# Attention, soft mixture and gated layer on one core: logit sums, combine products and batch-end steps on other engines and in other places

## The chip, the cores and the metric

One core of one Trainium2 chip runs the whole program in one launch. The metric is the device time of one execution in microseconds (us). The engines are named as the profile names them: PE is TensorE, which multiplies matrices (PEld is its weight load), DVE is VectorE, ACT is ScalarE, POOL is GpSimd, and SP is SyncE, whose queue issues the DMAs.

## What is computed

Three layers follow each other, all in float32. The input is q, k, v of 4 batches, 8 heads, 1152 positions, 64 wide; neighbouring pairs of queries are averaged first, so that 576 queries are left for each head.

```
q_pool = q.reshape(B, H, S // 2, 2, D).mean(axis=3)
attn = softmax(q_pool @ k.T / sqrt(D)); x = (attn @ v), heads side by side: 2304 x 512
logits = x @ phi                                  # phi: 512 x 32 slots
d = softmax over tokens of logits;  slot_input = d.T @ x
slot_out[e] = relu(slot_input[e] @ w1[e]) @ w2[e]  # 8 experts, 4 slots each
c = softmax over slots of logits (1e-9 added to the sum);  x = c @ slot_out
out = (silu(xn @ w_gate) * (xn @ w_val)) @ w_out   # xn: x over its rms, times rms_g
```

The part that the change touches is the softmax of the logits: `d` runs over all tokens and is made batch by batch with a running maximum, `c` runs over the 32 slots of one token.

## The kernel before, in words

The attention runs over 16 head pairs, p = 0 to 15, four to a batch; a stage is the work of one pair. Its loop has nine visits, kt = 0 to 8, one for each block of 128 keys. In a visit `qk` (L412) makes the scores of both halves (h = 0, 1) of the 288 + 288 queries on TensorE in four products, the last of which subtracts each query's maximum, and ScalarE makes the exponentials (L423). `add_e` (L428) adds the exponentials up on GpSimd in two accumulators a half (kt = 0 to 4 and 5 to 8), and `av` (L440) makes the output's products, three blocks of keys in every third visit. In p = 0 and 15 (`HALVED`) VectorE makes part of the sums, and the two halves follow each other. The maxima of later pairs are made in the same loop: `wide_item` (L354) makes scores on TensorE in a two-bank tile, VectorE reduces them.

All score-like results share one PSUM tag, `u`, of three two-bank tiles, which `two_banks` (L241) gives out; `bank` (L244) takes one of these for any smaller result too. A new tile takes the place of the one that was released longest ago in the order of the program, and waits until its last reader is done.

The order on each engine is written out by hand. `STEP` and `STEP_V` (L31, L32) list the steps of a visit (every third one is a `STEP_V`, of ten steps: scores q0 and q1, a maximum m, sums e0 and e1, the output's products a, b, c, with two more maxima between a and b). `side(p)` (L765) collects the steps at the side of a stage, each with a due time from `AT` (or `AT_0`, `AT_15` and `AT_01`, which replace some of its times in certain stages): a time of 5.46 means that the step's instructions are issued ahead of the first step of the visit kt = 5 that begins at 0.46 of it or later. So a due time sets the place of an instruction in the queue of its engine, and an engine takes its queue in order.

The steps at the side that matter here, for the pair l = p - 1 that has just been finished:

- `sum_up` (L456, due 0.1 and 0.11) adds the two accumulators of each half on VectorE. `turn_64` (L759, due 0.9, 5.76, 5.77) turns a 512-wide block of 64-bit weights into float32 on VectorE (L756). `sums` (L460, 2.75) adds over the keys on TensorE and ScalarE adds 1e-9; `recips` (L474) turns and inverts.
- `x_turn_all` (L499, 8.75) turns the outputs on TensorE; `x_divide` (L507, 8.76 and 8.77) divides them on VectorE. With `AT_01`, in stages with p > 1 and p % 4 < 2, these are due at 8.85 to 8.87.
- `x_logits` (L517, 5.45) makes the pair's share of the logits on TensorE in a `u` tile; `logit_mul` (L525, 5.46) divides it on VectorE; `logit_add` (L531, 6.3) adds it to the batch's logits on VectorE. It does so for the second to fourth pair of a batch: eleven times in the loop.
- `max_red` and `max_row` (L382, L385, 5.75 and 5.95) finish the maxima of the next pair and turn them to a row; `send_row` (L392, 6.0) sends it by DMA. `low_k` (L325, 6.1 and 6.2) makes the low part of the next keys on VectorE.
- At the end of a batch (p = 4, 8, 12) `d_turn` (L551) and `d_exp` (L578) make the exponentials over the tokens; for two halves VectorE then adds the two sums (L585). A stage later (p = 5, 9, 13) `d_back`, `d_copy`, `slot_part`, `slot_copy` and `slot_turn` (L587 to L633) follow. In p = 6, 10, 14 `c_turn` (L644) starts the combine's softmax of the batch, in p = 7, 11, 15 `c_exp` and `c_soft2` (L657, L660) end it: exponential on ScalarE; sum, addition of 1e-9 from the tile `eps`, inverse and product on VectorE. For the last batch these run ahead of the experts (L1130 to L1132).
- `pair_up` (L637, in p = 2) fills two constant tiles on VectorE.

After the loop come the last logits, the experts (L1014 on) and the gated layer (L1176 on), which TensorE fills almost alone.

Of the kernel before, what the change touches and what calls it, by code (L numbers as in the profile page):

```python
# [7 lines left out]
F32 = mybir.dt.float32  # L8
# [5 lines left out]
AF = mybir.ActivationFunctionType  # L14
ALU = mybir.AluOpType
# [3 lines left out]
NP = 16  # L19
# [31 lines left out]
    d_back=2.76,  # L51
    d_copy=2.77,
# [4 lines left out]
    c_soft=6.5,  # L57
# [9 lines left out]
    x_logits=5.45,  # L67
    logit_mul=5.46,
# [39 lines left out]
    take_x=0.24,  # L108
    sum_up=[0.25, 0.26],
# [52 lines left out]
def attention_softmoe_gated_kernel(ctx: ExitStack, tc: tile.TileContext, kT, qT, vv, ip, cst, w1, w2, wg, wv, wo, rg, out):  # L162
# [105 lines left out]
    eps = one.tile([TB, NBK], F32, name="eps")  # L268
# [262 lines left out]
    def logit_add(p):  # L531
        b, hp = divmod(p, 4)
        if hp:
            dv.tensor_tensor(out=lg[b], in0=lg[b], in1=srow[p], op=ALU.add)
        rel("B")
# [42 lines left out]
    def d_exp(g, o, nm):  # L578
        n = len(o)
        dtx[g] = B([32, 576], F32, "dtx")  # L580
        sm = S([32, 2], "sm")
        for h in range(n):
            ac.activation(dtx[g][:, HQ * h:HQ * h + HQ], o[h], AF.Exp, bias=nm, accum_out=sm[:, h:h + 1] if n > 1 else sall[:, g:g + 1])
        if n > 1:
            dv.tensor_tensor(out=sall[:, g:g + 1], in0=sm[:, 0:1], in1=sm[:, 1:2], op=ALU.add)  # L585
# [51 lines left out]
    def pair_up():  # L637
        dv.memset(pair, 0.0)
        dv.memset(eps, 1e-9)
        for h in range(2):  # L640
            r = slice(64 * h, 64 * h + 64)
            dv.tensor_copy(pair[r, h], stack[r, 0:32])
# [17 lines left out]
    def c_soft2(b):  # L660
        t = ct[b]
        sm = S([TB, NBK], "csm")
        dv.reduce_sum(out=sm, in_=t, axis=AX.X)
        dv.tensor_tensor(out=sm, in0=sm, in1=eps, op=ALU.add)
        dv.reciprocal(sm, sm)
        dv.tensor_tensor(out=cn[:, NBK * b:NBK * b + NBK, :], in0=t, in1=sm[:, :, None].to_broadcast([TB, NBK, 32]), op=ALU.mult)
# [98 lines left out]
    def side(p):  # L765
# [3 lines left out]
        def at(name, g):  # L769
            ts = (AT_0 if p == 0 else AT_15 if p == NP - 1 else AT_01 if p > 1 and p % 4 < 2 else AT).get(name, AT.get(name))  # L770
            for i, t in enumerate(ts if isinstance(ts, list) else [ts]):
                todo.append((t, len(todo), (lambda i=i: g(i))))
# [20 lines left out]
        if l >= 0:  # L793
# [14 lines left out]
            if p % 4 == 1 and p > 1:  # L808
                b = p // 4 - 1
                at("d_back", lambda i: d_back(b))  # L810
# [7 lines left out]
            if p % 4 == 3 and p > 3:  # L818
                b = p // 4 - 1
                at("c_exp", lambda i: c_exp(b))  # L820
                at("c_soft", lambda i: c_soft2(b))
# [27 lines left out]
    with tc.manual_schedule():  # L849
# [282 lines left out]
        c_soft2(3)  # L1132
# [216 lines left out]
```

## Time and profile before

| | us |
|---|---|
| median of 3 runs | 748.03 (747.66 to 750.51) |
| profiled execution | 744.76 |
| its span, first to last instruction | 742.9 |
| PE busy | 699.8 (94%) |
| DVE busy | 478.8 (64%) |
| POOL busy | 422.5 (57%) |
| ACT busy | 391.3 (53%) |

The span is read from the trace of the profiled execution; all times of single instructions are from it, in us from its first instruction. "Busy" counts the time in which an engine works on instructions; an instruction that has been started and is held up by another engine's access to the memory counts as busy, and so shows as a long instruction. The granted TensorE clock was 0.993 of the full one.

### The profile page before, as it was taken

What the parts mean: (1) busy time and instruction counts of PE and PEld (TensorE: products, weight loads), DVE (VectorE), ACT (ScalarE), POOL (GpSimd) and SP (SyncE); (2) the same over time, 40 slices, a digit from 0 to 9 for tenths busy, and PEclk for the clock granted to TensorE, in tenths of its full rate; (3) what the DMA queues carried; (4) which work ended last, traced back from release to release, by engine and by line L of the source; (5) the groups of instructions that cost most, each with busy time, mean ns of one, the idle gap of its engine ahead of it and who ended that gap; (6) DMA issues with size and microseconds to landing.
All of it is one profiled execution on the core that took longest, in us unless ns stands there. A gap on an engine that the chain in (4) does not pass through costs nothing.

```text
span 742.9 us, 15218 instructions
## 1 busy us (share of the span) xinstructions
PE 699.8 (94%) x5967; PEld 487.7 (66%) x5967; DVE 478.8 (64%) x691; ACT 391.3 (53%) x809; POOL 422.5 (57%) x340
## 2 busy tenths in 40 slices
PE   4999989899999899999999998989999999999998
PEld 2666656566666566666665665544357888888887
DVE  5968898887787887687897674432053755544420
ACT  2455656566656556565665543432155856554320
POOL 5336877876777677678777665221016854535330
PEclk9999999999999999999999999989999999999999
DMA  5221642844636617427416306079990010000001
GB/s 173 96 88 64 210 153 73 265 134 163 231 123 209 223 59 252 177 67 276 153 44 225 137 11 230 29 258 363 398 401 26 15 44 29 28 30 15 28 29 43
DMA packets 52855, 103.56 MB, mean 139 GB/s; under 512 B 5816, under 2 KB 19632, under 8 KB 52784
## 3 DMA queue, kind: packets, MB, share of 16 engines
q1 hardware_dynamic: 52784, 102.59, 39.6%
q8 instruction: 47, 0.77, 0.4%
q14 instruction: 24, 0.20, 0.1%
HBM read 89.39 MB, written 13.11 MB: 138 GB/s over the span
## 4 chain that ended last, share of the span: by engine, by line
PE 73%; DVE 13%; issue 5%; DMA 4%; ACT 3%; POOL 2%; SPq 0%; ACTq 0%; DVEq 0%; POOLq 0%
PE yo L1252 20%; PE sc L421 16%; PE av L444 15%; DVE mx L365 4%; PE mxp L364 4%; PE gv L1204 3%; DMA w<-away 2%; POOL acc L438 2%; DVE mx L371 2%; ACT e L423 2%; PE sums L469 1%; PE mxp L374 1%; PE hin L1021 1%; PE xl L521 1%; PE xo L504 1%
## 5 line engine op out<-in xcount | busy, mean ns | idle before, releaser
L438 POOL TENSOR_TENSOR acc<-acc,e 128x576 f32<-128x576 f32 x148 | 205.6, 1415 | 59.3 <-ACT e L423 49.9
L423 ACT ACTIVATE e<-sc 128x576 f32<-128x576 f32 x288 | 166.4, 657 | 93.2 <-PE sc L421 90.9
L365 DVE TENSOR_REDUCE mx<-mxp 128x2 f32<-128x1024 f32 x120 | 143.7, 1222 | 55.5 <-PE mxp L364 55.4
L444 PE MATMUL av<-e,vt 128*64 128x288 f32 x1152 | 165.2, 415 | 0.0
L438 POOL TENSOR_TENSOR acc<-e 128x576 f32<-128x576 f32 x60 | 91.9, 1549 | 95.3 <-ACT e L423 88.4
L444 PEld LDWEIGHTS av<-e,vt 128*64 128x64 f32 x1152 | 73.4, 136 | 60.5 <-issue 22.8
L421 PE MATMUL sc<-qh,kh 64*128 64x288 f32 x576 | 97.9, 329 | 3.6 <-DVE xt L513 2.8
L1252 PE MATMUL yo<-woh,hA 128*128 128x512 f32 (+1 forms) x312 | 98.9, 384 | 0.0
L421 PE MATMUL sc<-mr,pick 64*128 64x288 f32 x576 | 88.3, 294 | 1.5 <-DMA mr<-mrow 1.5
L421 PE MATMUL sc<-ql,kh 64*128 64x288 f32 x576 | 87.8, 294 | 0.0
L421 PE MATMUL sc<-qh,kl 64*128 64x288 f32 x576 | 87.7, 294 | 0.0
L1209 DVE SCALAR_TENSOR_TENSOR th<-th,gv 128x384 f32<-128x384 f32 x72 | 39.9, 554 | 62.5 <-ACT th L1206 61.9
L421 PEld LDWEIGHTS sc<-qh,kh 64*128 64x128 f32 x576 | 55.8, 185 | 28.9 <-issue 9.4
L1235 POOL TENSOR_TENSOR hA<-hu,hA 128x384 fp32r<-128x384 f32 x48 | 48.7, 1016 | 43.0 <-ACT hA L1234 39.3
L1252 PEld LDWEIGHTS yo<-woh,hA 128*128 128x128 f32 x312 | 57.6, 188 | 10.2 <-issue 0.7
L421 PEld LDWEIGHTS sc<-mr,pick 64*128 64x128 f32 x576 | 57.2, 187 | 1.9 <-DMA mr<-mrow 1.9
L1252 PE MATMUL yo<-wol,hA 128*128 128x512 f32 (+1 forms) x151 | 57.9, 383 | 0.0
L1206 ACT ACTIVATE th<-gv 128x384 f32<-128x384 f32 x72 | 35.2, 488 | 42.4 <-PE gv L1204 39.1
L421 PEld LDWEIGHTS sc<-qh,kl 64*128 64x128 f32 x576 | 57.1, 189 | 0.2
L421 PEld LDWEIGHTS sc<-ql,kh 64*128 64x128 f32 x576 | 56.9, 187 | 0.0
L364 PE MATMUL mxp<-kh,qh 64*128 64x512 f32 x240 | 49.1, 437 | 0.0
L1211 DVE SCALAR_TENSOR_TENSOR hu<-th,gv 128x384 f32<-128x384 f32 x72 | 39.9, 555 | 8.4 <-DVE th L1209 0.4
(201 smaller groups left out, 1070.9 us busy)
## 6 DMA issues: line engine op xcount, KB each, us to landing
w<-in_w_dram SPq DMA_DIRECT2D x86, 256.0 KB
w<-in_w_dram SPq DMA_DIRECT2D x21, 512.0 KB
vt<-in_vv_dram SPq DMA_DIRECT2D x16, 576.0 KB
qraw<-in_qT_dram SPq DMA_DIRECT2D x15, 576.0 KB
kraw<-in_kT_dram SPq DMA_DIRECT2D x15, 576.0 KB
away<-w SPq DMA_DIRECT2D x32, 256.0 KB
w<-away SPq DMA_DIRECT2D x32, 256.0 KB
raw<-in_wg_dram SPq DMA_DIRECT2D x12, 512.0 KB
```

What stands on the lines that cost most here:

```text
L364: pe.matmul(o[:, s, :], lhsT=q[r, 128 * t:128 * t + 128], rhs=k[r, 512 * c:512 * c + 512], start=True, stop=True)
L365: dv.reduce_max(out=heads[:, :, t, c], in_=o, axis=AX.X)
L421: pe.matmul(o[:, s, 0:HQ], lhsT=w[r, wk], rhs=q[r, c], start=(i == 0), stop=(i == 3))
L423: ac.activation(ets[p, kt, h], o[:, :, 0:HQ], AF.Exp, scale=0.0625)
L438: eng.tensor_tensor(out=acc[p, h, j], in0=first[p, h, j] if n == 1 else acc[p, h, j], in1=e, op=ALU.add)
L444: pe.matmul(avt[p, h][64 * s:64 * s + 64, 0:HQ], lhsT=vt[p][:, kt, 64 * s:64 * s + 64], rhs=ets[p, kt, h][:, s], start=(kt == 0), stop=(kt ...
L1204: pe.matmul(o[i], lhsT=sg[n][:, 256 * i + 128 * c:256 * i + 128 * c + 128], rhs=cT[g], start=True, stop=True)
L1206: ac.activation(t, o[0], AF.Tanh, scale=0.5)
L1209: dv.scalar_tensor_tensor(out=t, in0=t, scalar=1.0, in1=o[0], op0=ALU.add, op1=ALU.mult)
L1211: dv.scalar_tensor_tensor(out=u, in0=t, scalar=0.5, in1=o[1], op0=ALU.mult, op1=ALU.mult)
L1235: gp.tensor_tensor(out=b, in0=u, in1=f(a), op=ALU.subtract)
L1252: pe.matmul(o, lhsT=x, rhs=w[:, c], start=(ft == 0 and i == 0), stop=(ft == NF - 1 and i == 2))
```

## The change

The due times of eight steps change, `logit_add` and `pair_up` go from VectorE to GpSimd, the sum behind `d_exp` becomes a step `d_sum` of its own, and `c_soft2` becomes two steps: `c_sum`, in which ScalarE adds the 1e-9 between two instructions of VectorE, and `c_out`, the product, on GpSimd in the loop and on VectorE for the last batch. `AT_01` now holds in stages with p % 4 = 2 too.

```
 AT:     d_back 2.76 -> 2.81, d_copy 2.77 -> 2.82, new d_sum=2.8
         c_soft 6.5 -> [6.5, 8.9]
         x_logits 5.45 -> 5.78, logit_mul 5.46 -> 5.785
 AT_15:  new c_soft=[3.9, 4.6]
@@ logit_add
-            dv.tensor_tensor(out=lg[b], in0=lg[b], in1=srow[p], op=ALU.add)
+            gp.tensor_tensor(out=lg[b], in0=lg[b], in1=srow[p], op=ALU.add)
@@ d_exp
-        if n > 1:
-            dv.tensor_tensor(out=sall[:, g:g + 1], in0=sm[:, 0:1], in1=sm[:, 1:2], op=ALU.add)
+        dpart["s", g] = sm
+
+    def d_sum(g):
+        sm = dpart.pop(("s", g))
+        dv.tensor_tensor(out=sall[:, g:g + 1], in0=sm[:, 0:1], in1=sm[:, 1:2], op=ALU.add)
@@ pair_up
-        dv.memset(pair, 0.0)
-        dv.memset(eps, 1e-9)
+        gp.memset(pair, 0.0)
         for h in range(2):
             r = slice(64 * h, 64 * h + 64)
-            dv.tensor_copy(pair[r, h], stack[r, 0:32])
+            gp.tensor_copy(pair[r, h], stack[r, 0:32])
@@ c_soft2
-    def c_soft2(b):
-        t = ct[b]
-        sm = S([TB, NBK], "csm")
-        dv.reduce_sum(out=sm, in_=t, axis=AX.X)
-        dv.tensor_tensor(out=sm, in0=sm, in1=eps, op=ALU.add)
+    def c_sum(b):
+        sm = csum[b] = S([TB, NBK], "csm")
+        dv.reduce_sum(out=sm, in_=ct[b], axis=AX.X)
+        ac.activation(sm, sm, AF.Copy, bias=1e-9)
         dv.reciprocal(sm, sm)
-        dv.tensor_tensor(out=cn[:, NBK * b:NBK * b + NBK, :], in0=t, in1=sm[:, :, None].to_broadcast([TB, NBK, 32]), op=ALU.mult)
+
+    csum = {}
+
+    def c_out(b, eng=gp):
+        eng.tensor_tensor(out=cn[:, NBK * b:NBK * b + NBK, :], in0=ct[b], in1=csum[b][:, :, None].to_broadcast([TB, NBK, 32]), op=ALU.mult)
@@ side
-            ts = (... AT_01 if p > 1 and p % 4 < 2 else AT)...
+            ts = (... AT_01 if p > 1 and p % 4 < 3 else AT)...
             if p % 4 == 1 and p > 1:
+                at("d_sum", lambda i: d_sum(b))
             if p % 4 == 3 and p > 3:
-                at("c_soft", lambda i: c_soft2(b))
+                at("c_soft", lambda i: (c_sum, c_out)[i](b))
@@ ahead of the experts
-        c_soft2(3)
+        c_sum(3)
+        c_out(3, dv)
```

## Rows read from the trace of the kernel before

**Rows 1.** The page, part 1: busy us (share of the span) and instructions of each engine.

```profile
PE 699.8 (94%) x5967; PEld 487.7 (66%) x5967; DVE 478.8 (64%) x691; ACT 391.3 (53%) x809; POOL 422.5 (57%) x340
```

**Rows 2.** Waits of PE: who waited for whom: us in total, times, longest us.

```profile
PE xo L504 <- DVE mx L365: 5.9, 5, 2.3
...
PE mxt L388 <- DVE mxw L383: 4.1, 13, 1.0
PE sums L469 <- DVE acc L457: 2.9, 2, 1.7
PE sums L469 <- DVE mx L365: 2.9, 2, 2.4
PE sc L421 <- DVE xt L513: 2.8, 3, 0.9
...
PE dn L591 <- DVE mx L365: 1.4, 3, 0.5
```

**Rows 3.** Groups of instructions on DVE, shapes apart: count | busy us, mean ns | idle before.

```profile
L534 DVE TENSOR_TENSOR lg<-lg,srow 128x288 f32<-128x288 f32 x11 | 14.9, 1355 | 0.0
...
L529 DVE TENSOR_TENSOR srow<-xl,srow 128x288 f32<-128x288 f32 x11 | 4.9, 448 | 0.0
...
L666 DVE TENSOR_TENSOR cn<-ct,csm 96x192 f32<-96x192 f32 x4 | 4.2, 1050 | 0.1
...
L642 DVE COPY pair<-cs 64x32 f32<-64x32 f32 x2 | 2.6, 1278 | 0.0
```

**Rows 4.** Timeline of DVE, p = 6, kt = 5 and 6: start us, us, instruction [idle before].

```profile
211.73 1.23 DVE L365 TENSOR_REDUCE mx<-mxp 128x2 f32<-128x1024 f32 x1 [0.57 <-PE mxp L364]
...
214.12 0.18 DVE L383 TENSOR_REDUCE mxw<-mx 128x9 f32<-128x27 f32 x1
214.22 1.28 DVE L756 SCALAR_TENSOR_TENSOR w<-w,raw 128x512 uint32<-128x512 uint32 x2
215.42 1.42 DVE L328 TENSOR_TENSOR kl<-kraw,kh 128x576 fp32r<-128x576 f32 x2
216.76 1.69 DVE L534 TENSOR_TENSOR lg<-lg,srow 128x288 f32<-128x288 f32 x1
```

**Rows 5.** Timeline of POOL, p = 6: the two accumulations of kt = 6.

```profile
216.25 3.46 POOL L438 TENSOR_TENSOR acc<-e 128x576 f32<-128x576 f32 x2 [3.21 <-ACT e L423]
```

**Rows 6.** Timeline of POOL, first accumulations of p = 2, 3, 4, 5, 7, 8, 12.

```profile
82.56 3.39 POOL L438 TENSOR_TENSOR acc<-e 128x576 f32<-128x576 f32 x2 [1.19 <-ACT e L423]
...
112.00 2.80 POOL L438 TENSOR_TENSOR acc<-e 128x576 f32<-128x576 f32 x2 [2.90 <-ACT e L423]
...
138.59 3.47 POOL L438 TENSOR_TENSOR acc<-e 128x576 f32<-128x576 f32 x2 [0.51 <-ACT e L423]
...
169.75 2.90 POOL L438 TENSOR_TENSOR acc<-e 128x576 f32<-128x576 f32 x2 [2.65 <-ACT e L423]
...
227.14 2.80 POOL L438 TENSOR_TENSOR acc<-e 128x576 f32<-128x576 f32 x2 [1.96 <-ACT e L423]
...
256.10 2.80 POOL L438 TENSOR_TENSOR acc<-e 128x576 f32<-128x576 f32 x2 [2.84 <-ACT e L423]
...
369.35 3.29 POOL L438 TENSOR_TENSOR acc<-e 128x576 f32<-128x576 f32 x2 [1.44 <-ACT e L423]
```

**Rows 7.** Timeline of PE, p = 6: output products a, the turned maxima, scores of kt = 6.

```profile
210.11 1.14 PE L444 MATMUL av<-e,vt 128*64 128x288 f32 x8
...
214.45 0.30 PE L388 MATMUL mxt<-cs,mxw 128*128 128x128 f32 x1 [0.27 <-DVE mxw L383]
...
215.32 0.29 PE L421 MATMUL sc<-qh,kh 64*128 64x288 f32 x2
```

**Rows 8.** Timeline of DVE, end of p = 4.

```profile
166.44 0.66 DVE L585 TENSOR_TENSOR sall<-sm 32x1 f32<-32x1 f32 x1 [1.19 <-ACT dtx L583]
```

**Rows 9.** Groups on POOL, shapes apart: the sum of 192 columns.

```profile
L877 POOL TENSOR_TENSOR qs<-qraw 128x192 f32<-128x192 f32 x1 | 0.6, 589 | 1.1 <-DMA qraw<-in_qT_dram 1.1
```

**Rows 10.** Timeline of ACT, p = 7, kt = 6 to 8: the exponentials.

```profile
243.50 3.41 ACT L423 ACTIVATE e<-sc 128x576 f32<-128x576 f32 x6 [0.47 <-PE sc L421]
```

More of the change, by code (lines that the diff above doesn't have):

```diff
@@ L50 @@
     sums=2.75,
-    d_back=2.76,
-    d_copy=2.77,
+    d_sum=2.8,
+    d_back=2.81,
+    d_copy=2.82,
     max_tail=[2.85, 2.86],
@@ L56 @@
     c_exp=0.9,
-    c_soft=6.5,
+    c_soft=[6.5, 8.9],
     pair_up=6.6,
@@ L66 @@
     slot_copy=5.77,
-    x_logits=5.45,
-    logit_mul=5.46,
+    x_logits=5.78,
+    logit_mul=5.785,
     logit_add=6.3,
@@ L108 @@
     take_x=0.24,
+    c_soft=[3.9, 4.6],
     sum_up=[0.25, 0.26],
@@ L267, in attention_softmoe_gated_kernel @@
     pair = one.tile([128, 2, 32], F32, name="pair")
-    eps = one.tile([TB, NBK], F32, name="eps")
     rgt = one.tile([128, 4], F32, name="rgt")
@@ L769, in at @@
         def at(name, g):
-            ts = (AT_0 if p == 0 else AT_15 if p == NP - 1 else AT_01 if p > 1 and p % 4 < 2 else AT).get(name, AT.get(name))
+            ts = (AT_0 if p == 0 else AT_15 if p == NP - 1 else AT_01 if p > 1 and p % 4 < 3 else AT).get(name, AT.get(name))
             for i, t in enumerate(ts if isinstance(ts, list) else [ts]):
```

## The prediction

> **What bounds the kernel now.** I read the page first: TensorE is busy for 94% of the span, VectorE and GpSimd for 64% and 57% [rows 1]. So the time is TensorE's own work plus the gaps in it, and a change that touches only the other engines can win no more than the gaps. I then read who makes TensorE wait [rows 2]. In the sixteen stages of the attention (one a head pair, p = 0 to 15) the gaps made by VectorE are: the turned outputs, 5.9 in five gaps (2.2 in p = 2, 2.3 in p = 7, 0.44, 0.44 and 0.49 in p = 6, 10, 11); the turned maxima, 4.1 in thirteen; the sums, 2.9 behind a maximum (2.4 in p = 4, 0.5 in p = 2) and 2.9 behind the accumulators' sum in p = 15; the scores behind x_divide, 2.8 in three (p = 5, 9, 13); d_back, 1.4 in the same three.
>
> Next I asked why VectorE is late. Eight of the eleven logit sums take 1.69 and three 0.45, the two copies of pair_up 1.28 each, the combine's product 1.05 on average [rows 3]. In p = 6, GpSimd's accumulation starts 0.5 us ahead of the slow sum, and the sum ends 0.3 after it [rows 4, 5]; that accumulation and the next one last 3.46 together, where two alone take 2.80 (p = 3) [rows 5, 6]. So the engines hold each other up a whole instruction at a time, and the one that waits goes next. VectorE's time is lost to GpSimd's sums, and the change trades this one way for the other.
>
> The last view is the start of each stage. VectorE adds the accumulators as soon as GpSimd has made its last one, then turns a weight (0.64, as in [rows 4]), and only then makes the maxima that TensorE's sums wait for. GpSimd starts on the new stage when the second exponentials are there; the idle time before that is the room VectorE has [rows 6]. The accumulators' sum is two instructions of 0.7. A room of 1.4 holds both, and the weight gets in ahead of GpSimd: in p = 12 the room is 1.44 and TensorE waits for nothing. In p = 2 it is 1.19, the weight comes behind one of GpSimd's sums, and TensorE waits 0.5. In p = 4 it is 0.51, the second instruction comes behind GpSimd too, and TensorE waits 2.4. So the limits are about 1.4 and 0.7.
>
> **The change, part by part** (us; plus is longer).
>
> Gaps that go. The 2.2 in p = 2 goes: the sum (1.69) and pair_up (its copies 2.6, and the memsets) leave VectorE. The 2.3 and 0.49 in p = 7 and 11 go: VectorE is rid of the sum, the addition of 1e-9 and the product. The two 0.44 in p = 6 and 10 go, as x_turn stands eight matmul instructions of the output products, or 1.1, later [rows 7]. Sum -5.9. In p = 5, 9, 13 VectorE no longer waits 1.19 for the exponentials and 0.66 in the tiny d_sum [rows 8], 1.85 against gaps of 0.93: -2.8. There d_back too stands behind 1.1 more of products, against gaps of 0.47: -1.4. The moved d_sum (0.66) is covered by the time in which TensorE makes d_back and then the products of VectorE's next maximum; uncovered it would cost its 0.66 three times. No DMA is moved: send_row, load_v and SP's queue keep their places, and the row leaves 0.3 earlier.
>
> Logits behind the maxima. TensorE no longer makes xl ahead of the last maxima, so VectorE's idle 0.57 goes and the maxima end 0.57 earlier. The gap of 0.27 ahead of the turned maxima goes in eleven stages: -2.9. But xl takes one of three score buffers, and the second pair of scores of kt = 6 now needs it back, behind the product, which stands behind max_red and two weights. In p = 6: the product starts at 215.42 - 0.57 = 214.85, ends 0.45 later at 215.30 [rows 3, 4], and with 0.14 to signal (as from mxw to mxt) the scores start at 215.44. TensorE would be there 0.27 ahead of the 215.32 of before [rows 7], so it waits 0.39. Eight stages turn two weights there: +3.1. With one weight (p = 1, 11, 14) the product is 0.6 earlier: nothing. In p = 5, 9, 13 slot_part's sixteen matmul instructions stand ahead of xl and give VectorE time: nothing there (at most the 0.39).
>
> Logits' sum on GpSimd. The trace has no such sum; GpSimd's sums take 0.59 at 192 columns and 1.40 at 576 [rows 6, 9]; in proportion between them 288 columns take 0.79. These are the bounds, and I take 0.79. It waits behind the product, and the accumulation of kt = 6 waits behind it. It becomes ready during the first low_k (0.71 each), so it goes between the two: the second low_k and that accumulation come 0.79 - 0.12 = 0.67 later. GpSimd no longer waits 0.3 for VectorE's sum, so its last accumulation ends 0.35 to 0.45 later, TensorE's scores 0.12 later: the room of the next stage shrinks by 0.3.
>
> By the Trainium skill, GPSIMD Engine Reference, section 4.1 (Engine selection), an elementwise sum belongs on VectorE, GpSimd being about twice as slow with two inputs. By that the sum would take 0.90 and the room would shrink by a further 0.1, worth some 0.2 in the total.
>
> Combine. In p = 7 and 11 VectorE makes the sum, ScalarE adds 1e-9, VectorE inverts. ScalarE would come to its copy after two of the six exponentials that now run back to back [rows 10], at 244.65; VectorE ends its sum behind both low_k, in p = 7 at 243.28 (product) + 0.71 + 0.79 + 0.71 + 0.34, or 245.8. So the exponentials behind the copy are held 1.3, three score buffers run full, and TensorE stands for it (VectorE's inverse waits too, but only the maxima of kt = 8 queue behind it, whose products come later): +1.3 in p = 7, +1.1 in p = 11, where one weight is turned. If low_k were not split it would be 0.45 each. In p = 15, where both have idle time, nothing (at most the 1.3). The product itself (0.59 by the 192-column sum, up to 1.0) goes to GpSimd behind its last accumulation, and the accumulators' sum waits for it: 0.6 less room in p = 8 and 12. In the experts' phase the same hop stands against an addition and a product that held VectorE up: nothing, within 0.3 either way.
>
> What is late next: the rooms. GpSimd's work behind kt = 6 is one unbroken row of accumulations, so whatever TensorE stops waiting there comes off the next room:
> - p = 3: 2.90 - 0.3 - 2.2 - 0.7 for pair_up on GpSimd (three small instructions without a row, between nothing and three times 0.59; I take 0.7, nearer the low end as they are 32 and 64 columns wide) is below zero. GpSimd goes straight on, and a third instruction of VectorE's comes behind one of its sums, 1.4 to 2.0 more than the 2.4: 3.8 to 4.4. With pair_up at nothing a room of 0.4 is left and the wait is 2.4. I take 3.6.
> - p = 4: 0.51 - 0.3, still above zero: the 2.4 becomes 2.75, +0.35. In p = 15 TensorE waits for the accumulators' sum itself, and GpSimd ends 0.3 later: +0.3.
> - p = 5, 9, 13 (2.65 or 2.66): 2.65 - 0.93 - 0.3 is 1.4, on the limit: half of 0.5 each, +0.7.
> - p = 7, 11 (both 1.96): 1.96 - 0.3 - 0.44 is 1.2: +1.0 for both.
> - p = 8: 2.84 - 0.3 - 2.3 + 1.3 - 0.6 is 0.9; p = 12: 1.44 - 0.3 - 0.5 + 0.8 - 0.6 is 0.9: +1.0 for both.
> Sum +7.0.
>
> **The sum.** -5.9 - 2.8 - 1.4 - 2.9 is -13.0; +3.1 + 2.4 + 7.0 is +12.5; together -0.5. The profiled execution took 744.76 (span 742.9), which would become 744.3. The runs shown have a median of 748.03, 3.3 above it, so I forecast 747.5 for such a median.
>
> **The rivals.**
> Faster: the rooms hold. If GpSimd's sum fits into its idle 3.2 ahead of kt = 6 without parting the low_k, the rooms lose only TensorE's gaps: p = 5, 7, 9, 11, 13 keep 1.5 and more and lose nothing (-1.7), p = 4 and 15 neither (-0.65), ScalarE is held 0.9 in place of 2.4 (-1.5), p = 3 ends at the lower 2.4 (-1.2). That is -5.1 in all, 742.4. For it: the idle 3.2 is there. Against: the sum is only ready when low_k has begun.
> Slower: GpSimd becomes the bound. If its sum costs 1.3, as accumulations do, in place of 0.79, the rooms lose 0.5 more: p = 7, 8, 11 and 12 fall to 0.7 or below, where the wait is 2.4 in place of 0.5 (+7.6), p = 5, 9, 13 pass the limit (+0.7): 755.8. It decides from a sum of about 1.0, where p = 8 and 12 pass 0.7 (+3.8 for the two). For it: p = 4 and 15 show the price today. Against: the narrow sum of [rows 9]. The Trainium skill's rule above points this way; it has no chance beside this rival's.
> Neutral by another road: TensorE's gaps go, but the scores' buffer and ScalarE's copy cost nothing because other work slips in; then the rooms of p = 8 and 12 fall below 0.7 by what TensorE didn't wait, and gaps of 2.4 stand there in place of 0.5: -3.1 - 2.4 + 3.8, 745.8, inside the forecast's 0.5%.
>
> **How the numbers follow.** A measurement of this kernel tells about 0.5%, 3.7 us, from no change. I give 0.50 to an end within it (the forecast and its neutral neighbour), 0.30 to faster, 0.20 to slower. The likeliest case by itself runs from 744.1 to 749.0, by nothing or 0.5 for each room on the limit, 2.4 or 4.4 in p = 3, 0.9 or 2.4 for ScalarE. The range goes on to 741 (the faster case with nothing lost in p = 3 would give 740) and to 753.5, which leaves out about one in ten on either side.
>
> **What would show it.** Right: no gap of the turned outputs above 0.5, none of the scores behind x_divide, none ahead of the turned maxima; in their place scores of kt = 6 waiting for VectorE's product, scores in p = 7 and 11 waiting for ScalarE's exponentials by a microsecond, and sums waiting for VectorE in p = 3 by about 3 and in p = 7, 8, 11, 12 by a half. GpSimd's idle time before the first accumulation of p = 3 would be gone. Wrong: the sum of TensorE's gaps falls by over 4 (GpSimd took its work for nothing), or the sums' gaps are 2 and more in five or more stages.

## The result, and the profile after

The changed kernel takes 753.12 us (median of 20 executions, 751.07 to 755.14), the kernel before 748.91 on the same chip (20 executions, 743.48 to 753.02). The ratio is 1.0053, with a 95% interval of 1.0032 to 1.0074: slower by about 4 us, a loss that is clear of noise. The forecast was 747.5, or half a microsecond less than before. The profiled execution after took 753.1 (span 751.2, granted clock 0.977); the one before 744.76 (742.9, 0.993). Single executions of some runs below were disturbed (740 us became 1400 or more); the medians and ratios below leave them out, so that a time quoted in an expectation can be up to 0.8 above the one given here.

Lines of the code have moved down by 1 to 8, so the scores are L422, the sums L470, the logits' sum L535. The page of the changed kernel, part 1, answers to [rows 1]:

```profile
PE 707.9 (94%) x5967; PEld 491.4 (65%) x5967; DVE 475.8 (63%) x669; ACT 391.6 (52%) x813; POOL 443.5 (59%) x357
```

The waits of TensorE in the changed kernel (us in total, times, longest) answer to [rows 2]:

```profile
PE sums L470 <- DVE mx L366: 14.0, 10, 4.5
...
PE sums L470 <- DVE acc L458: 3.0, 2, 1.9
...
PE c4o L1072 <- DVE c L1066: 1.8, 1, 1.8
PE sc L422 <- ACT e L424: 1.6, 2, 1.1
...
PE mxt L389 <- DVE mxw L384: 1.2, 2, 1.0
```

The waits for xo (5.9), of the scores behind x_divide (2.8), of d_back (1.4) and 2.9 of the 4.1 of the turned maxima are gone. In their place the sums wait 14.0 for VectorE's maxima, where it was 2.9: 4.53 in p = 3, 4.15 in p = 4 and 0.6 to 0.7 in eight other stages. So the gaps nearly balance, as forecast. But TensorE is busy 8.1 us longer (707.9 against 699.8) with the same 5967 instructions, and no gap explains that.

The windows of the stages p = 3, p = 4, p = 15 and of all that follows the last exponential show it, first of the kernel before (window, its length, busy time and instructions of each engine, granted TensorE clock, DMA):

```profile
110.19:136.77 26.58, 26.27 (x269) 18.08 (x269) 21.91 (x27) 17.38 (x33) 20.13 (x15) 1.00 0.39 126
136.77:166.89 30.12, 27.38 (x275) 18.20 (x273) 25.15 (x29) 18.04 (x38) 23.59 (x16) 1.00 0.57 190
...
451.81:484.51 32.70, 28.93 (x264) 17.45 (x264) 14.70 (x26) 14.44 (x28) 9.65 (x7) 1.00 0.28 106
484.51:742.87 258.36, 248.75 (x1601) 186.85 (x1597) 105.39 (x217) 117.07 (x279) 96.20 (x98) 0.99 0.33 123
```

The same windows of the changed kernel:

```profile
107.71:139.93 32.22, 27.69 (x270) 18.42 (x269) 24.87 (x26) 17.25 (x33) 24.26 (x17) 0.95 0.39 127
139.93:173.85 33.92, 29.77 (x277) 19.38 (x275) 25.83 (x29) 17.99 (x37) 24.97 (x18) 0.90 0.51 168
...
454.76:490.39 35.63, 31.63 (x265) 18.47 (x264) 13.72 (x23) 14.69 (x29) 11.16 (x9) 0.90 0.27 98
490.39:751.24 260.85, 250.76 (x1601) 188.08 (x1597) 105.36 (x216) 117.36 (x279) 96.37 (x98) 0.97 0.34 122
```

The same work of TensorE takes 1.42, 2.39, 2.70 and 2.01 longer in these four windows, 8.5 together, and in each the granted clock is lower. Two windows of the changed kernel are at half clock (0.50, the 1.2 GHz level). Each begins before the long wait of its stage ends (the sums start at 116.85 and 148.69) and runs on behind it:

```profile
116.80:120.00 3.20, 3.15 (x16) 0.97 (x16) 2.25 (x2) 1.52 (x3) 1.47 (x2) 0.50 0.95 285
...
147.30:154.10 6.80, 5.41 (x24) 2.59 (x26) 4.51 (x5) 1.52 (x3) 2.82 (x2) 0.50 0.82 266
```

The last two windows of the list can't be charged to the change by one pair of profiles. In p = 15 the waits are nearly the same before and after (2.9 and 3.0 in two). Eight of the profiles of this document have them: six of these show a half clock there, among them both of the kernel before with one edit each ("The weight out of the way" and "The logits alone"), and two show none, the kernel before and the changed kernel with `pair_up` put back. The window of p = 15 in the kernel before with the late weight, then in the changed kernel with `pair_up` put back:

```profile
454.00:489.28 35.28, 31.52 (x266) 18.45 (x264) 14.78 (x26) 14.47 (x28) 9.66 (x7) 0.90 0.28 98
...
450.17:483.11 32.94, 28.94 (x266) 17.45 (x264) 13.64 (x23) 14.66 (x29) 11.16 (x9) 1.00 0.28 97
```

So there it comes and goes by chance. The 24 executions of the kernel before in one later session run from 743.42 at a granted clock of 0.995 to 753.49 at 0.982, and its profile shown above is near the lower end. So the pair of profiles differs by 8.3 and the medians by 4.2. p = 3 and p = 4 remain.

Why the sums wait so long is in the timelines of the changed kernel around the start of p = 3 (107.71), GpSimd's first:

```profile
99.41 1.25 POOL L535 TENSOR_TENSOR lg<-lg,srow 128x288 f32<-128x288 f32 x1 [2.31 <-DVE srow L530]
100.60 0.15 POOL L642 MEMSET pair<- 128x64 f32 x1
100.82 0.78 POOL L645 COPY pair<-cs 64x32 f32<-64x32 f32 x2
...
109.92 3.32 POOL L439 TENSOR_TENSOR acc<-e 128x576 f32<-128x576 f32 x2
```

VectorE's timeline of the same stretch:

```profile
99.24 2.03 DVE L329 TENSOR_TENSOR kl<-kraw,kh 128x576 fp32r<-128x576 f32 x2
...
110.01 3.84 DVE L458 TENSOR_TENSOR acc<-acc 128x576 f32<-128x576 f32 x2 [3.10 <-POOL acc L439]
113.77 1.88 DVE L762 SCALAR_TENSOR_TENSOR w<-w,raw 128x512 uint32<-128x512 uint32 x1
115.58 3.48 DVE L366 TENSOR_REDUCE mx<-mxp 128x2 f32<-128x1024 f32 x3
```

GpSimd's first accumulation of the stage has no idle time before it (it had 2.90 in [rows 6]). So, as the rows read, each instruction of VectorE's with two inputs comes behind one of GpSimd's: the accumulators' sum takes 3.84 where two alone take 1.4, the weight 1.88 where it takes 0.64. The maxima start at 115.58 and TensorE's sums at 116.85, after 4.53 of waiting.

### The profile page after: what moved, and what is told of

It reads as the page before. It is cut to its first block, busy times and chain, and to the rows that moved or that the text cites. A ratio compares the mean times of both kernels' runs of the same rounds, so it can differ in the third digit from the quotient of the medians.

```text
span 751.2 us, 15203 instructions
## 1 busy us (share of the span) xinstructions
PE 707.9 (94%) x5967; PEld 491.4 (65%) x5967; DVE 475.8 (63%) x669; ACT 391.6 (52%) x813; POOL 443.5 (59%) x357
## 4 chain that ended last, share of the span: by engine, by line
PE 66%; DVE 10%; issue 9%; POOL 7%; DMA 4%; ACT 3%; SPq 1%; ACTq 0%; POOLq 0%; DVEq 0%
PE yo L1260 20%; PE sc L422 13%; PE av L445 13%; POOL acc L439 6%; PE gv L1212 3%; DVE w L762 3%; DVE mx L366 3%; PE mxp L365 2%; DMA w<-away 2%; PE sums L470 2%; PE hin L1028 2%; ACT e L424 2%; DVE acc L458 2%; DMA kraw<-in_kT_dram 1%; PE mxp L375 1%
## 5 line engine op out<-in xcount | busy, mean ns | idle before, releaser
L445 PE MATMUL av<-e,vt 128*64 128x288 f32 x1152 | 169.5, 422 | 0.0
L439 POOL TENSOR_TENSOR acc<-e 128x576 f32<-128x576 f32 x60 | 96.2, 1621 | 47.6 <-ACT e L424 47.5
L422 PE MATMUL sc<-qh,kh 64*128 64x288 f32 x576 | 97.6, 332 | 2.5 <-ACT e L424 1.6
L422 PE MATMUL sc<-mr,pick 64*128 64x288 f32 x576 | 87.4, 295 | 1.5 <-DMA mr<-mrow 1.5
L422 PE MATMUL sc<-qh,kl 64*128 64x288 f32 x576 | 87.0, 295 | 0.0
L422 PE MATMUL sc<-ql,kh 64*128 64x288 f32 x576 | 87.0, 295 | 0.0
L422 PEld LDWEIGHTS sc<-qh,kh 64*128 64x128 f32 x576 | 55.4, 186 | 28.6 <-issue 10.1
L422 PEld LDWEIGHTS sc<-mr,pick 64*128 64x128 f32 x576 | 56.4, 188 | 1.9 <-DMA mr<-mrow 1.9
L422 PEld LDWEIGHTS sc<-qh,kl 64*128 64x128 f32 x576 | 56.4, 190 | 0.3
L422 PEld LDWEIGHTS sc<-ql,kh 64*128 64x128 f32 x576 | 56.1, 188 | 0.0
```

The costliest lines, as they stand in the source:

```text
L422: pe.matmul(o[:, s, 0:HQ], lhsT=w[r, wk], rhs=q[r, c], start=(i == 0), stop=(i == 3))
L439: eng.tensor_tensor(out=acc[p, h, j], in0=first[p, h, j] if n == 1 else acc[p, h, j], in1=e, op=ALU.add)
L445: pe.matmul(avt[p, h][64 * s:64 * s + 64, 0:HQ], lhsT=vt[p][:, kt, 64 * s:64 * s + 64], rhs=ets[p, kt, h][:, s], start=(kt == 0), stop=(kt ...
```

## The experiments

The theory: the change's gains and costs in TensorE's gaps cancel, as forecast; the loss is the granted clock, which falls to half behind the long waits that the change makes in p = 3 and p = 4. The rivals: GpSimd's added work is the loss by itself, whatever the clock; or the half clock comes and goes by chance, and the waits have no part in it. All ratios are to the kernel before, run on the same chip in the same session; its median was 747.6 to 748.3.

**TensorE kept at work in the two waits.** Unread products stand ahead of the sums; nothing else differs from the changed kernel.

```
+    def fill(p):
+        for _ in range(20):
+            pe.matmul(avt[p, 0][:, 288:512], lhsT=kh[p][:, 0:128], rhs=kh[p][:, 0:224], start=False, stop=False)
...
+            if p in (3, 4):
+                at("fill", lambda i: fill(p))    # due 2.74, sums 2.75
```

> Leaves nothing out: 20 products whose results nobody reads stand ahead of the sums in p = 3 and p = 4, so that TensorE works through its two longest waits (4.53 and 4.15 us). Theory (the change's own terms cancel, the loss is TensorE's clock, which was granted at half behind those two waits): the sums come no earlier, but the clock stays at 1.0 from p = 3 to p = 5 and the time falls by 3 to 4 us against the changed kernel, to about 749.5. Rival (GpSimd's added work is the loss and the clock has no part in it): the same 753 as the changed kernel, or more by what the products cost.

749.74, ratio 1.0010 [0.9981, 1.0039]. p = 4 fell from 33.92 to 31.56 at a clock of 1.00, although its sums come no earlier and 1.8 of the wait was left; p = 3 (2.1 of its wait left) stayed at 0.95 and at 32.36. The time is as expected; the half clock that stays in p = 3 isn't. The same with 36 products in p = 3 and 32 in p = 4:

> The changed kernel with the same unread products of 288 to 511 columns ahead of the sums, now 36 in p = 3 and 32 in p = 4 (20 in each left 2.1 and 1.8 of the two waits, and the half clock behind p = 3's). What they compute is never read; nothing else differs. The clock theory: with 36 the wait of p = 3 falls to about 0.8 and that of p = 4 to about 0.6, no stretch at half clock is left at 117 us nor at 147 us, and stage p = 3 is about 1.4 shorter than the 32.23 of the changed kernel although the sums come no earlier; p = 4 stays near the 31.56 that 20 products gave. The time falls to about 748, against 749.7 with 20. The rival, in which the half clock comes by itself and the wait has no part in it: a half-clock stretch stays at 117 us, p = 3 stays near 32.3, the time near 749.7. The rival, in which GpSimd's added work is the whole loss: GpSimd does the same work here, so the time stays at 753.

749.30, ratio 1.0018 [0.9994, 1.0043]. The same version again, for its profile:

> The version with 36 and 32 unread products in p = 3 and 4 once more, since a profile of an undisturbed execution is wanted. The clock theory: no half clock at 117 nor at 147 us, stage p = 3 near 30.8 and p = 4 near 31.6. The time was 749.4, only 0.3 below that with 20 products where 1.4 was expected: if p = 3 is still at half clock there, or another stretch has taken its place, the stages of the profile say which.

749.18, ratio 1.0006 [0.9975, 1.0036]; the windows of p = 3 and p = 4:

```profile
109.13:140.00 30.87, 30.50 (x306) 22.12 (x305) 24.91 (x26) 17.39 (x34) 24.35 (x17) 1.00 0.42 132
140.00:171.56 31.56, 31.14 (x307) 21.97 (x307) 25.86 (x29) 18.16 (x37) 25.02 (x18) 1.00 0.54 181
```

TensorE does more and both stages are shorter: 32.22 and 33.92 became 30.87 and 31.56, or 3.7 less, at a clock of 1.00. The sums come as late as before, 9.19 and 8.80 behind the start of the stage against 9.14 and 8.76, so all of the gain lies behind them. GpSimd is busy as long as before (24.35 and 25.02 against 24.26 and 24.97). That is the loss: with the clock kept, the changed kernel is level with the kernel before. The rival of GpSimd's work falls, since it would have left 753. The rival of chance falls for these two stages: 17 of the 20 executions of the changed kernel had a mean clock of 0.977, and none of the 31 with products was below 0.979 (the ten of the last run 0.984 to 0.989). The step from 20 to 36 products brought less in the median (0.4 to 0.6) than the 1.4 expected, a difference that these intervals, some 2 us to either side, don't resolve.

**The price of a wait by itself.** In the mixed version (below, 732.5), whose stages p = 4, 8, 12 wait 0.7, 0 and 0 at full clock, VectorE makes four unread maxima ahead of its own.

```
+    def hold(p):                                   # in p = 4, 8, 12, due 1.2
+        for _ in range(4):
+            t = S([128, 1], "hold")
+            dv.reduce_max(out=t, in_=kh[p][:, 0:1024], axis=AX.X)
```

> Measures the price of a long wait of TensorE by itself, in the mixed version (732.5, whose stages p = 4, 8 and 12 hold waits of 0.7, 0 and 0 us and no half clock): in these three stages VectorE makes four unread maxima over 1024 columns ahead of its own (about 1.1 to 1.2 each, 4.6 in all), so that TensorE's sums wait some 3.5 to 5 longer. The maxima go to a scratch tile that nothing reads; no other part differs. If a wait costs its own length and no more, the time is 732.5 plus the waits that the profile shows in the three stages, 743 to 747. If TensorE is granted half its clock behind such a wait, a stretch of 3.4 or 6.8 us at half clock follows each of the three waits, as in p = 4 of the changed kernel, and each costs 1.7 to 3.4 on top: 748 to 757.

747.95, ratio 0.9986 [0.9959, 1.0014]. TensorE's timeline of this run has the waits of the sums in p = 8 and in p = 12:

```profile
259.50 0.69 PE L471 MATMUL sums<-acc,ones 128*32 128x288 f32 x8 [3.32 <-DVE mx L367]
...
374.46 0.69 PE L471 MATMUL sums<-acc,ones 128*32 128x288 f32 x8 [3.33 <-DVE mx L367]
```

The windows of the two stages:

```profile
251.57:283.78 32.21, 28.89 (x277) 19.17 (x275) 27.56 (x33) 18.01 (x37) 23.34 (x18) 0.95 0.42 140
366.53:397.17 30.64, 27.32 (x277) 18.40 (x275) 27.42 (x33) 18.01 (x38) 23.37 (x18) 1.00 0.35 112
```

The same wait, 3.3, costs 3.4 in p = 12 (30.64 against 27.24 in the mixed version) and 4.96 in p = 8 (32.21 against 27.25), where a stretch at half clock follows it (260.2 to 263.6). p = 4, with a wait of 2.9, is at 0.95 too. So a wait brings the half clock often, not always: 1.6 each time it does. By their length alone the waits in the profile (9.6 against 0.7) would have made 741.4, and the two half clocks 744.5. Of the 3.4 that are left up to 747.95 the profile has 0.9 in p = 3 and 1.4 behind the last exponential; the rest isn't taken apart. With 34 unread products in the waits:

> The same as the run with the unread maxima in p = 4, 8 and 12, and ahead of the sums of these stages 34 products of 224 columns into columns of the output tile that nobody reads, some 0.11 to 0.12 us each, 4 us in all: TensorE works where it waited, the sums come no earlier. If a wait costs only its length, this is as slow as the run without the products, or slower by as much as the products run past the maxima. If the clock behind the wait is the further cost, the half-clock stretches behind the three stages are gone and this is 5 to 10 faster than the run without the products, though it does more.

745.54, ratio 0.9945 [0.9915, 0.9974]: 2.4 faster, not the 5 to 10 expected. The windows of p = 8 and p = 12:

```profile
251.97:283.21 31.24, 31.24 (x310) 22.26 (x309) 27.44 (x33) 18.01 (x37) 23.43 (x18) 1.00 0.42 142
366.00:397.23 31.23, 31.23 (x309) 22.27 (x309) 27.42 (x33) 18.02 (x37) 23.43 (x18) 1.00 0.35 111
```

These two stages are the clean comparison. In both the products fill the wait (none is left) and run on past it. p = 12, which had no half clock, got 0.59 longer by that (31.23 against 30.64); p = 8, which had one, got 0.97 shorter (31.24 against 32.21) though it does more. Had the wait of p = 8 cost only its length, both would have got longer. The 2.4 of the whole can't be put down to the three stages: together they are 0.5 longer in this profile (95.09 against 94.63), since in p = 4 GpSimd's idle time ahead of its first accumulation was 0.32 in place of 1.44, VectorE's sum of the accumulators took 2.65 in place of 1.43, and TensorE's sums came 2.3 later. What got shorter is p = 3 (a wait of 0.9 for a maximum is gone) and what follows p = 14 (1.9, with less half clock behind the last exponential); neither is the products' doing as far as the traces show.

**The weight out of the way.** `turn_64` of the start of a stage is made at 4.6 in place of 0.9, in the changed kernel and in the kernel before.

```
-    turn_64=[0.9, 5.76, 5.77],
+    turn_64=[4.6, 5.76, 5.77],
```

> The changed kernel with the first turned weight of a stage due at 4.6 in place of 0.9, so that it no longer stands between the accumulators' sum and the maxima. Theory: the eight waits of 0.6 to 0.7 ahead of the sums (p = 2, 5, 7, 8, 9, 11, 12, 13) go, some 5.4 us; the waits of p = 3 and 4 lose one GpSimd instruction each (1.5 to 1.9), to 2.3 to 3.0, and the half clock behind them goes (about 3.8): 741 to 744. Rival (GpSimd's work is the bound): its work is the same, so the time stays within 2 us of 753.

> The kernel before with the first weight of a stage turned at 4.6 in place of 0.9, nothing of the change in it. It tells whether the gain of 10.6 that this gave in the changed kernel belongs to the weight alone or to the weight together with the smaller rooms. By the theory of rooms the weight only costs where it comes behind one of GpSimd's sums: before, that is p = 2 (0.5) and p = 4 (about 0.7 to 1.8 of 2.4), so the gain is 1 to 2.5: 746 to 747.5, and the change with the late weight (742.5) is ahead of it by 4 to 5. By the rival, in which the change does nothing but lose and the weight's place by itself is the gain: about 738, ahead of the changed kernel with the late weight.

In the changed kernel 741.65, ratio 0.9907 [0.9871, 0.9943]: all waits of 0.6 to 0.7 are gone, p = 3 waits 2.71 and p = 4 2.35, p = 1 waits 1.68 for a maximum. The time is as expected, but the half clock behind the waits of p = 3 and p = 4 didn't go (the stages are at 0.94 and 0.95); it is only shorter in p = 4. In the kernel before 747.07, ratio 1.0005 [0.9976, 1.0033]: the 2.4 in p = 4 fell to 0.56 and the 0.48 in p = 2 went, but 1.5 came in p = 1. The ratio shows no gain where 1 to 2.5 was forecast, though its interval reaches 1.8, and the rival (738) is far off. By the weight alone nothing is won; the changed kernel with it is ahead by 5.4 between the medians and 0.0098 in the ratio, since the gaps that the change closes stay closed and most of their price in the rooms goes.

**Parts of the change undone.** First `pair_up`, then the logits' sum, is put back on VectorE in the changed kernel.

```
-        gp.memset(pair, 0.0)
+        dv.memset(pair, 0.0)
...
-            gp.tensor_copy(pair[r, h], stack[r, 0:32])
+            dv.tensor_copy(pair[r, h], stack[r, 0:32])
```

> The changed kernel with pair_up back on VectorE. Theory: GpSimd ends p = 2 some 0.6 us earlier, the wait of p = 3 falls from 4.5 to 2.4 to 3.0, the half clock behind it goes (1.4): 749.5 to 751, p = 4 unchanged. Rival (pair_up's place has no part in it, the logits' sum alone sets the rooms): wait of p = 3 still over 4, time 753.

746.63, ratio 0.9972 [0.9943, 1.0001], 3 better than expected. p = 3 waits 0.77, not the 2.4 to 3.0 expected, in place of 4.53, for 0.36 of xo in p = 2: GpSimd's idle time ahead of its first accumulation is 0.84, where it was nothing. p = 4 keeps its 4.15. That p = 15 is at full clock in this profile, as shown above, is worth 2.7 more in it.

```
-            gp.tensor_tensor(out=lg[b], in0=lg[b], in1=srow[p], op=ALU.add)
+            dv.tensor_tensor(out=lg[b], in0=lg[b], in1=srow[p], op=ALU.add)
```

> The changed kernel with the logits' sum back on VectorE at 6.3. Theory: the rooms of the stages behind p = 2, 3, 4, 6, 7, 8, 10, 11, 12 grow by 0.3; p = 4 waits 2.5 to 2.8 in place of 4.15 and keeps its clock (-1.4 - 2.4), p = 5, 9, 13 come to the limit (0 to -0.7 each), while VectorE's longer sum costs up to 1 in p = 7: 747 to 750. Rival (the sum's engine doesn't matter, the places do): 752 to 754.

741.5, ratio 0.9906 [0.9871, 0.9941], 5 and more better than expected. p = 3 waits 2.46, p = 4 2.56, p = 8 and 12 nothing, p = 15 1.46 in place of 3.01; the scores wait 3.6 for ScalarE in p = 7 and 11 (1.6 after the change). The idle time of GpSimd at the start of p = 5 and p = 7 is 1.36 and 1.39, where the changed kernel has 1.00 and 0.98, and at that TensorE's sums don't wait there. p = 4 didn't keep its clock as expected: half clocks stand behind the waits of p = 3 and 4, and one behind the 2.1 for ScalarE in p = 7. All waits for the sums together fell by 9.9, while those for ScalarE rose by 2.0. By the Trainium skill, GPSIMD Engine Reference, section 4.1 (Engine selection), an elementwise sum belongs on VectorE and not on GpSimd; the run agrees, with a ratio of 0.9906 against 1.0053, or 11 us. What it costs, though, isn't the sum's own length (1.21 on average against 1.36 before), but the stage that GpSimd ends later.

**The logits alone.** The kernel before, with `x_logits` at 5.78 and `logit_mul` at 5.785 and nothing else.

```
-    x_logits=5.45, logit_mul=5.46,
+    x_logits=5.78, logit_mul=5.785,
```

> The kernel before with one part of the change: the pair's share of the logits made at 5.78 and divided at 5.785, behind the maxima, and nothing else moved. By the forecast's step the turned maxima lose their gaps (-2.9) and the second scores of kt = 6 wait 0.39 for the product that holds their buffer in eight stages (+3.1): about 0 in all, with eight waits of sc for VectorE's product in the list. By the present theory those scores take the buffer of the turned maxima, and not that of the product: no such wait, -2.9 in the gaps, of which some 0.5 to 1.5 comes back where a room is at its limit (p = 2 and p = 4 by 0.3 each, p = 12 by 0.5): 746 to 747 against 748.3. The waits in the list tell the two apart, not the time.

749.36, ratio 1.0012 [0.9984, 1.0039], above the 746 to 747 expected. Its waits of TensorE, to be held against [rows 2]:

```profile
PE xo L504 <- DVE mx L365: 7.7, 5, 2.5
...
PE sc L421 <- DVE xt L513: 3.3, 3, 1.1
PE sums L469 <- DVE mx L365: 3.1, 2, 2.6
...
PE mxt L388 <- DVE mxw L383: 1.2, 2, 1.0
```

The 2.9 of the turned maxima went and no scores wait for the product, as the present theory has it; but 2.5 came back at once, 1.8 of it with xo (1.91 in p = 11, where it was 0.49), 0.5 in the scores behind x_divide, 0.2 in the sums. Half clocks stand in its profile behind three of these waits (2.44 in p = 2, 2.57 in p = 4, 1.91 in p = 11) and none behind a fourth (2.49 in p = 7). The gain of the logits' place is only kept where VectorE is relieved as well.

**Versions that beat both kernels.** Mixed: the changed kernel with the late weight, `pair_up` on VectorE, and the logits' sum on VectorE for l = 2 and 13 only.

```
+            (dv if p in (2, 13) else gp).tensor_tensor(out=lg[b], in0=lg[b], in1=srow[p], op=ALU.add)
```

> A version meant to beat both kernels: the changed kernel with the first weight of a stage turned at 4.6 in place of 0.9 (this alone gave 742.5), pair_up back on VectorE (this alone gave 746.6 and took the wait of p = 3 from 4.5 to 0.9), and the sum of the logits on VectorE for l = 2 and 13 only, the pairs ahead of the rooms of p = 4's and p = 15's stages. By the theory of rooms: p = 3 waits 0.3 or less, p = 4 under 1.5 in place of 4.15, p = 15 about 1.5 in place of 3.0, no stage a 0.6 to 0.7; ScalarE's 1.1 and 0.5 in p = 7 and 11 stay; by the clock theory no half clock is left at 117 and 147 us, since no wait above 2 stands there. Time 735 to 739. If GpSimd's sum of the logits is what costs, by itself, the version with it on VectorE in all stages (741.5) is not beaten by more than 1.

732.47, ratio 0.9798 [0.9769, 0.9826], better than the 735 to 739 expected: p = 3 doesn't wait for its sums, p = 4 waits 0.73, p = 15 1.49, no other sums wait, and no half clock stands in p = 3, 4 or 15. Next, the 1e-9 back on VectorE and the weight of p = 1 early:

```
-        ac.activation(sm, sm, AF.Copy, bias=1e-9)
+        dv.tensor_tensor(out=sm, in0=sm, in1=eps, op=ALU.add)
...
+            if name == "turn_64" and p == 1:
+                ts = [0.9, 5.76, 5.77]
```

> A version meant to be faster still than the mixed one (732.5): the late weight stays early (0.9) in p = 1 alone, where the late place made TensorE wait 1.7 for a maximum, and the 1e-9 of the combine's sum is added on VectorE again as before the change, without the way over ScalarE. Expected: the wait of xl for the maximum in p = 1 falls to about 0.3 (-1.4), and the waits of the scores for ScalarE in p = 7 and 11, 1.1 and 0.5, go (-1.6), which also gives the true size of the forecast's term of +2.4 for that way. 729 to 730. If the addition on VectorE costs a whole instruction of GpSimd's sums there, the waits come back as sums or scores behind VectorE, and the time stays at 731 or above.

737.10, ratio 0.9833 [0.9807, 0.9859]: slower than mixed by 4.6. The waits for ScalarE (1.1 and 0.5) and the 1.4 in p = 1 went as expected, but the sums of p = 8 now wait 6.83, and those of p = 12 0.83. GpSimd's timeline at the start of p = 8 in the mixed version:

```profile
247.75 0.50 POOL L672 TENSOR_TENSOR cn<-ct,csm 96x192 f32<-96x192 f32 x1
249.13 3.08 POOL L439 TENSOR_TENSOR acc<-e 128x576 f32<-128x576 f32 x2 [0.88 <-ACT e L424]
```

VectorE's there:

```profile
247.81 1.73 DVE L458 TENSOR_TENSOR acc<-acc 128x576 f32<-128x576 f32 x2 [1.15 <-POOL acc L439]
```

GpSimd's timeline at the same place in this version:

```profile
245.54 0.51 POOL L674 TENSOR_TENSOR cn<-ct,csm 96x192 f32<-96x192 f32 x1
246.01 2.80 POOL L440 TENSOR_TENSOR acc<-e 128x576 f32<-128x576 f32 x2
248.75 1.44 POOL L309 TENSOR_TENSOR qs<-qraw 128x576 f32<-128x576 f32 x1
250.12 2.77 POOL L440 TENSOR_TENSOR acc<-acc,e 128x576 f32<-128x576 f32 x2
```

VectorE's there:

```profile
245.63 8.55 DVE L459 TENSOR_TENSOR acc<-acc 128x576 f32<-128x576 f32 x2 [2.37 <-POOL acc L440]
```

Without the hold-up by ScalarE TensorE comes to p = 8 a microsecond earlier, the room of 0.88 is 0.0, and VectorE's two instructions take 8.55, nearly all of it in the first (7.88). To tell the room from the addition, GpSimd is relieved in p = 7 and 11:

```
-            (dv if p in (2, 13) else gp).tensor_tensor(out=lg[b], ...)
+            (dv if p in (2, 6, 10, 13) else gp).tensor_tensor(out=lg[b], ...)
+            if p % 4 == 0 and p > 4:
+                at("c_late", lambda i: c_out(l // 4 - 1))     # due 5.5, in place of 8.9 a stage earlier
```

> The version that reached 737.1 with a wait of 6.8 in p = 8, its 1e-9 still added on VectorE, but GpSimd relieved ahead of the stages p = 8 and 12: the combine's product moves from the end of p = 7 and 11 to the middle of p = 8 and 12 (0.5 each), and the logits' sums of l = 6 and 10 are made on VectorE (0.55 of room each). By the theory of rooms GpSimd's idle time ahead of the first accumulation of p = 8 is back at 0.7 to 0.8, VectorE's two instructions of the accumulators' sum take under 3 in place of 8.55, and the sums of p = 8 wait 0.7 or less (2.4 at the worst): 729 to 732. If the addition on VectorE itself is the cause, the 6.8 stays in p = 8, and the time near 737.

730.23, ratio 0.9758 [0.9727, 0.9788]. The 6.83 is gone, with the addition still on VectorE, and the room of p = 8 is 1.56, more than the 0.7 to 0.8 expected. GpSimd's timeline at the start of p = 8:

```profile
246.31 2.81 POOL L441 TENSOR_TENSOR acc<-e 128x576 f32<-128x576 f32 x2 [1.56 <-ACT e L426]
```

VectorE's there:

```profile
244.78 1.43 DVE L460 TENSOR_TENSOR acc<-acc 128x576 f32<-128x576 f32 x2 [0.97 <-POOL acc L441]
```

So the addition isn't the cause. Part of the gain went back as xo in p = 7 (1.15) and 11 (0.54), with the logits' sum on VectorE there; a wait of TensorE there makes the room larger too, so how much of the 1.56 GpSimd's relief gave isn't shown. Last, mixed with only the weight of p = 1 early:

> The mixed version (732.5) with the late weight kept early, at 0.9, in p = 1 alone, and nothing else; ScalarE still adds the 1e-9. Expected: the wait of xl in p = 1 falls from 1.7 to 0.3, all else stays as in the mixed version, waits of p = 8 none, since ScalarE holds TensorE 1.1 in p = 7 and the room of p = 8 stays at 0.9: 731.0, or 1.4 less than the mixed version. A wait of several us in p = 8 here would say that the addition on VectorE was not its cause, nor the end of p = 7.

731.59, ratio 0.9779 [0.9743, 0.9814]. The wait in p = 1 fell from 1.67 to 0.28, and p = 8 has none, as expected; the ratio is 0.0019 below that of the mixed version, or the 1.4 expected, though no more than the intervals allow by chance. In the profile p = 0 was 1.5 longer with the same waits, as TensorE ran at half pace for longer at its start (the record of the granted clock begins only behind it). The same twelve output products take 3.06 there (from 22.56) and 1.68 in the mixed version (from 22.10).

## Why the prediction was wrong

**The step that failed** is the one that the whole sum rests on: "the time is TensorE's own work plus the gaps in it". It took TensorE's own work as given, and put the cost of the clock at nothing without a reason. Behind the 4.53 of p = 3 and the 4.15 of p = 4 that work was granted half its clock, which cost 3.7 in the profile, about the difference between the ratios 1.0053 and 1.0006 (3.5). The forecast held both waits in its hands, 3.6 and 2.75, and priced them at their length. None of its signs of being right or wrong looks at the clock, and neither of its signs of being wrong came. By its own terms the sum was close: the kernel with the clock kept in these two stages (1.0006, with 2 us of doubt to either side) is half a microsecond slower than before, against -0.5 forecast. But that the terms met there was partly luck:

- **Gaps that go**, -13.0: right to the tenth (5.9, 2.8, 1.4 and 2.9 are gone).
- **The scores' buffer**, +3.1: nothing. In p = 6 of the changed kernel the scores of both halves of kt = 6 run without a gap, while VectorE's product, whose buffer the second were to wait for, ends at 221.21. VectorE's timeline:

```profile
220.76 0.45 DVE L530 TENSOR_TENSOR srow<-xl,srow 128x288 f32<-128x288 f32 x1
```

TensorE's:

```profile
219.93 0.33 PE L389 MATMUL mxt<-cs,mxw 128*128 128x128 f32 x1
220.20 0.40 PE L422 MATMUL sc<-qh,kh 64*128 64x288 f32 x2
...
220.70 0.30 PE L422 MATMUL sc<-mr,pick 64*128 64x288 f32 x2
220.83 0.30 PE L422 MATMUL sc<-qh,kh 64*128 64x288 f32 x2
```

  The second scores start at 220.83, ahead of the product's end. So they aren't in the buffer that it reads, and the forecast's count of which buffer comes free next was wrong.
- **ScalarE's copy**, +2.4: 1.6 (1.1 and 0.5). That such a hold-up also covers a room worth 6.8 was seen only when it was taken out of the mixed version.
- **The rooms**, +7.0: 11.3. p = 3 cost 4.53 (3.6), p = 4 1.75 more (0.35), p = 5, 9 and 13 together 2.08 (0.7), p = 7 and 11 1.39 (1.0), p = 8 and 12 1.29 (1.0), p = 2 and 15 0.1 each (0 and 0.3). The mechanism was right: every stage whose room fell below the limit of 1.4, to 0.86 to 1.07, pays 0.6 to 0.7. The size was off: the logits' sum takes 1.21 on GpSimd (0.79 taken), and beside TensorE's gaps that went the rooms shrank by some 0.55 in p = 7 and 11 and 0.7 in p = 5, 9 and 13, not 0.3. That put p = 4, which had 0.51, at nothing, where the forecast had it "still above zero", and p = 5, forecast on the limit at 1.4, below it. The first accumulations of p = 4 and p = 5 in GpSimd's timeline of the changed kernel:

```profile
141.76 3.33 POOL L439 TENSOR_TENSOR acc<-e 128x576 f32<-128x576 f32 x2
...
175.63 3.58 POOL L439 TENSOR_TENSOR acc<-e 128x576 f32<-128x576 f32 x2 [1.00 <-ACT e L424]
```

  For the room of p = 12 the forecast counted 0.8 of hold-up, where its own text has 1.1 for p = 11; between its limits both give the same price. Its "the one that waits goes next" held in its own rows, but not always: in p = 8, above, VectorE's first instruction waited through five of GpSimd's.
- **The experts' phase**, within 0.3: +0.3 (c4o waits 1.77 for VectorE, 1.43 before).

The waits that came (11.3 + 1.6 + 0.3) against the 13.0 that went give +0.2; two misses, 4.3 too little for the rooms and 3.9 too much for buffer and ScalarE, cancelled.

Of the rivals, the slower one had the right sign and the wrong cause. Its point was a sum on GpSimd of about 1.0, from which p = 8 and 12 would fall to 0.7 and pay 2.4 each. The sum is 1.21, yet the rooms of p = 8 and 12 are 0.87 and 0.86, and they pay 0.65 and 0.64. The neutral one's step, that a stall which goes takes its stage's next room with it, is what happened in p = 8 when ScalarE's copy was taken out of the mixed version, at 6.8 in place of 2.4.

## What to carry to other kernels

A gap on a busy TensorE is not priced at its length. Those of 2.4 to 4.5 us here cost a third to two thirds as much again where the clock fell behind them, and those of 0.6 to 0.8 that stood alone didn't; two short ones close together did (p = 1, below). So several short gaps well apart are better than one long one of the same sum, and a long wait that can't be removed may be filled with unread products, as long as they end with the wait. Where two engines hold each other up by whole instructions, look for the idle time in front of the first instruction of each stage: while it is there VectorE's work is cheap, and at zero the next two instructions took 3.8 to 8.6 us here. A stall that looks like pure loss can be the cover of such a room, so remove it last, and with the room's price in the sum. And one profile of a kernel can lie 4 us off its median by the clock alone: look at the clock of each stage before two profiles are compared.

## What the runs showed of the hardware

- The granted clock of 0.50 followed waits of TensorE for its sums of 2.1 (p = 3 with 20 products), 2.35 (p = 4 with the late weight), 2.46 and 2.56 (p = 3 and 4 with the logits' sum back), 2.71, 2.91, 3.3, 4.15 and 4.53 us. The 2.40 in p = 4 of the profile before, the 1.8 in p = 4 with 20 products and one of the two of 3.3 were followed by none, nor was the wait of 2.3 for xo in p = 7 of the profile before. Two waits close together brought it too: 0.9 and 0.6 for a DMA in p = 1 in 12 of the 15 profiles, the kernel before among them, and 1.8 and 1.1 in p = 15 in six of eight; a single 1.5 in p = 15 in none of seven. The kernel before varies with it from 743.4 (0.995) to 753.5 (0.982) with nothing changed.
- Two instructions of VectorE's took 8.55 while GpSimd ran without a break, where they take 1.43 alone. The Trainium skill, SBUF — State Buffer, section "SBUF: two separate sides", says that the port pair which the two share is locked for a whole instruction and the loser waits for all of it; the rows agree, and show more than one lost turn for an instruction: 8.55 less 1.43 leaves 7.1, or five instructions of 1.4, and GpSimd's timeline has five in a row there.
- GpSimd's two copies of 64 by 32 took 0.78 together, the same on VectorE 2.6 [rows 3], and its product of 192 columns 0.50 against 1.05: so moving a small instruction to GpSimd can shorten it. That VectorE's are long here because they are held up is argued from their place among GpSimd's, and no run has them alone.
